# A fixed order of instructions for the first eleven head pairs of a fused attention, gate and mixer kernel

## The chip, the cores and the metric

One core of one Trainium2 chip runs the whole program. The metric is the device time of one execution in microseconds (us): the median of 3 executions of the kernel before is 831.82 us (831.67 to 832.71).

## What is computed

Three blocks follow each other, all in float32 (weights arrive as float64 words). B = 4, 12 heads, S = 448, head size 64, model width 768.

```python
scores = scale * np.matmul(q, k.transpose(0, 1, 3, 2)) - np.log(S)
attn = 1.0 / (1.0 + np.exp(-scores))              # a sigmoid, no row sums
x = np.matmul(attn, v)                            # heads side by side: (B, S, 768)
gate_pre += conv_w[k][None, None, :] * xp[:, k:k + S, :]     # 5 causal taps
x = (1.0 / (1.0 + np.exp(-gate_pre))) * (x @ w_val) @ w_out
h = np.maximum(x.transpose(0, 2, 1) @ w_tok1, 0.0) @ w_tok2
u = x + h.transpose(0, 2, 1)
out = u + np.maximum(u @ w_ch1, 0.0) @ w_ch2
```

## The kernel before

The heads are worked on in pairs: 24 pairs, six to a batch. For pair i, `scores` (L201) multiplies k by q in four chunks (8 matmuls in the program; the trace counts each as two) into a PSUM tile `pss` of which there are two, and ScalarE turns each chunk into a sigmoid tile `a` (L209, 128x896, four buffers). `av` (L212) multiplies v by the four chunks into `psy`, ScalarE copies the result to `x` (L221), and a DMA stores it to a scratch in device memory (L222). `x_back` (L224) loads it again as `xb`, with four columns of padding in front, two buffers. `post_pair` (L230) then makes of `xb` two things: its two halves in the reduced float32 format that the dense matmuls read (`split`, L88: high part on ScalarE L89, low part on VectorE L95), and the gate before its sigmoid: one tap on ScalarE (L237), four on VectorE (L239), the sigmoid at L243.

The weights are decoded on the chip. `fetch` loads 768 KB of float64 words as `raw` (three buffers), and `decode` (L104) makes a high and a low part of them in eight steps: two masks and a sum on VectorE (L110, L112, L113), a rebase of the exponent on ScalarE (L111), a merge on VectorE (L116), the high part on ScalarE (L119), an exponent mask and the low part on VectorE (L120, L121). Eighteen tiles are decoded in this phase: six of w_val, six of w_out (128x768), four of w_tok1 (128x256) and two of w_tok2 (128x448). The convolution's 30 columns `cw` are decoded as well. The tiles `dec_a` have two buffers, `dec_c` has one.

The order on each engine comes from a scheduler: it takes the instructions in the order in which they are written as priorities, models their times, and fills an engine's gaps with whatever is ready in its model. On the chip each engine then runs its list strictly in order. `PLAN` (L24) says what is written beside which pairs: pairs 0 to 10 stand alone (the lead), then the projections of batch 0 (`dense_steps`) are woven between the pairs from 11 on. `DEC_AT` (L33) says how many tiles are decoded at each pair:

```python
DEC_AT = (1, 1, 1, 1, 1, 1, 0, 0, 0, 0, 1, 2, 2, 2, 3, 2)
POST_FROM = 5
```

Behind the pairs come the channel mixer's matmuls (`ch1`, L479, and `ch2`, L491), the largest part of the program.

Of the kernel before, what the change touches and what calls it, by code (L numbers as in the profile page):

```python
# [31 lines left out]

DEC_AT = (1, 1, 1, 1, 1, 1, 0, 0, 0, 0, 1, 2, 2, 2, 3, 2)  # L33

# [4 lines left out]
def tile_kernel(ctx, tc, qT, kT, v, w_val, conv_w, w_out, w_tok1, w_tok2, w_ch1, w_ch2, out):  # L39
# [36 lines left out]
    def f(ap):  # L76
        return ap.bitcast(F32)
# [25 lines left out]

    def decode(pool, n, raw, h_out, l_out):  # L104
# [3 lines left out]
        a = pool.tile([P, DC], I32, tag="dec_a", bufs=2, name="dec_a")[:, :n]  # L108
        c = pool.tile([P, DC], I32, tag="dec_c", bufs=1, name="dec_c")[:, :n]
        nc.vector.tensor_scalar(out=a, in0=hi, scalar1=0x7FFFFE00, scalar2=None, op0=ALU.bitwise_and)  # L110
        nc.scalar.activation(out=a, in_=a, func=AF.Relu, scale=8.0, bias=exp_b)  # L111
        nc.vector.tensor_scalar(out=c, in0=hi, scalar1=0x1FF, scalar2=None, op0=ALU.bitwise_and)  # L112
        nc.vector.scalar_tensor_tensor(  # L113
            out=c.bitcast(F32), in0=lo.bitcast(U32), scalar=2.0**-32, in1=c, op0=ALU.mult, op1=ALU.add
        )
        nc.vector.scalar_tensor_tensor(  # L116
            out=a, in0=hi, scalar=-0x80000000, in1=a, op0=ALU.bitwise_and, op1=ALU.bitwise_or
        )
        nc.scalar.activation(out=h_out, in_=a.bitcast(F32), func=AF.Copy)  # L119
        nc.vector.tensor_scalar(out=e, in0=a, scalar1=-0x800000, scalar2=None, op0=ALU.bitwise_and)  # L120
        nc.vector.scalar_tensor_tensor(  # L121
            out=l_out, in0=c.bitcast(F32), scalar=2.0**-20, in1=e.bitcast(F32), op0=ALU.mult, op1=ALU.mult
        )

# [20 lines left out]
    def dec_conv(pool):  # L145
        n = KD * KW

        def go(raw):
            h = attn.tile([P, n], F32R, tag="cwHL", bufs=1, name="cwH")
            lo = attn.tile([P, n], F32R, tag="cwL", bufs=1, name="cwL")  # L150
            decode(pool, n, raw, h, lo)
            nc.vector.tensor_tensor(out=cw, in0=f(h), in1=f(lo), op=ALU.add)

        return (lambda raw: nc.gpsimd.dma_start(raw, conv_w.bitcast(I32))), go

    def dec_tok1(pool, c):
# [7 lines left out]

        return ld, lambda raw: decode(pool, NTOK, raw, wt1H[:, c], wt1L[:, c])

    def dec_tok2(pool, c):
        def ld(raw):
            nc.gpsimd.dma_start(raw[:, : 2 * S], w_tok2[c * P : (c + 1) * P].bitcast(I32))

        return ld, lambda raw: decode(pool, S, raw, wt2H[:, c], wt2L[:, c])

    def dec_w(pool, sel, kk):
# [11 lines left out]

    def load_pair(i):
        b, p = divmod(i, NP)
# [11 lines left out]
        raw_t[i] = (q, k, t)  # L199

# [28 lines left out]

    def post_pair(i):  # L230
        p = i % NP
        x = x_t.pop(i)
        xs = both.tile([P, 2, S], F32R, tag="xs", bufs=7, name="xs")
        split(xs[:, 0], xs[:, 1], x[:, PAD:])
        xs_t[i] = xs
        acc = both.tile([P, S], F32, tag="gate", bufs=6, name="gate")
        nc.scalar.activation(out=acc, in_=x[:, :S], func=AF.Copy, scale=cw[:, p * KW : p * KW + 1])  # L237
        for t in range(1, KW):
            nc.vector.scalar_tensor_tensor(  # L239
                out=acc, in0=x[:, t : t + S], scalar=cw[:, p * KW + t : p * KW + t + 1], in1=acc,  # L240
                op0=ALU.mult, op1=ALU.add,
            )
        nc.scalar.activation(out=acc, in_=acc, func=AF.Sigmoid)  # L243
        gate_t[i] = acc

# [116 lines left out]
    def dec_go():  # L362
        if raws:
            raw, go = raws.pop(0)
            go(raw)
            dec_load()

    load_pair(0)
    dec_load()
    load_pair(1)  # L370
    dec_load()
    dec_load()
    craw = attn.tile([P, 2 * KD * KW], I32, tag="craw", bufs=1, name="craw")
# [35 lines left out]

    for c in range(NF + 1):  # L410
        scores(0, c)
    rest_of = {}
    pairs0 = PLAN[0][2]
    for b, parts, pairs in PLAN:
        weave(1.0)
# [12 lines left out]
        for n, i in enumerate(pairs):  # L428
# [14 lines left out]
            post(2 if i > pairs0[-1] else 1 if i >= POST_FROM else 0)  # L443
            weave((n + 1.0) / len(pairs))
# [145 lines left out]
```

## Time and profile before

| | |
|---|---|
| median of 3 executions | 831.82 us |
| the profiled execution, its own time | 832.21 us |
| its span (first to last instruction) | 830.3 us |
| TensorE (PE) matmuls busy | 792.5 us, 95% of the span |
| VectorE (DVE) busy | 373.8 us, 45% |
| ScalarE (ACT) busy | 295.2 us, 36% |
| moved by DMA | 80.49 MB, mean 97 GB/s |

The page also cuts the span into 40 slices of 20.8 us and gives the busy share of each engine in tenths. PE has 7, 7, 6, 8, 8, 9 and then nothing but 9 until the end; VectorE has 5, 9, 7, 9, 7 and then at most 6 for a long time; the granted TensorE clock is 9 in nearly all slices, 8 in the third and the fifth.

An engine's row in the timeline gives start, duration, engine, line, operation, out<-in, count, and in brackets how long the engine stood idle before it and what ended that. Rows of one engine overlap a little, since a new instruction starts while the last one drains; what an instruction costs its engine in a dense row is the distance to the next start.

### The profile page before, as it was taken

What the parts mean: (1) busy time and instruction counts of PE and PEld (TensorE: products, weight loads), DVE (VectorE), ACT (ScalarE), POOL (GpSimd) and SP (SyncE); (2) the same over time, 40 slices, a digit from 0 to 9 for tenths busy, and PEclk for the clock granted to TensorE, in tenths of its full rate; (3) what the DMA queues carried; (4) which work ended last, traced back from release to release, by engine and by line L of the source; (5) the groups of instructions that cost most, each with busy time, mean ns of one, the idle gap of its engine ahead of it and who ended that gap; (6) DMA issues with size and microseconds to landing.
All of it is one profiled execution on the core that took longest, in us unless ns stands there. A gap on an engine that the chain in (4) does not pass through costs nothing.

```text
span 830.3 us, 9671 instructions
## 1 busy us (share of the span) xinstructions
PE 792.5 (95%) x3776; PEld 614.3 (74%) x3776; DVE 373.8 (45%) x635; ACT 295.2 (36%) x440; POOL 34.2 (4%) x97
## 2 busy tenths in 40 slices
PE   7768899999999999999989999999999999999998
PEld 2222236567677767777978899889999999999997
DVE  5979705431265323634479589994001200030002
ACT  6768755543435433433144244451002000020000
POOL 1111100000000000000000100000000000000000
PEclk9989899999999999999999999999999999999999
DMA  8756642221213121103254244535000500041001
GB/s 277 250 187 213 180 133 78 83 69 42 96 57 100 56 67 51 46 16 120 75 191 133 77 161 156 174 131 196 1 1 14 187 0 1 1 155 35 0 1 67
DMA packets 50686, 80.49 MB, mean 97 GB/s; under 512 B 4544, under 2 KB 46032, under 8 KB 50640
## 3 DMA queue, kind: packets, MB, share of 16 engines
q1 hardware_dynamic: 47280, 65.29, 24.3%
q0 software_dynamic: 3360, 14.58, 5.2%
q8 instruction: 30, 0.49, 0.2%
q14 instruction: 16, 0.13, 0.1%
HBM read 63.34 MB, written 16.52 MB: 96 GB/s over the span
## 4 chain that ended last, share of the span: by engine, by line
PE 75%; DVE 13%; DMA 6%; issue 3%; ACT 2%; SPq 1%; POOL 0%; DVEq 0%; POOLq 0%; ACTq 0%
PE psd L264 20%; PE psh L484 18%; PE pso L498 16%; PE pss L207 7%; PE psy L219 7%; PE pst L303 3%; PE pst L316 3%; DMA raw<-w_ch 3%; DVE dec_a L116 2%; DVE dec_c L113 2%; DVE wch L121 1%; DMA raw<-w_val 1%; DVE dec_a L110 1%; DVE raw L120 1%; DVE dec_c L112 1%
## 5 line engine op out<-in xcount | busy, mean ns | idle before, releaser
L484 PE MATMUL psh<-us,wch 128*128 128x448 f32 x864 | 184.6, 366 | 0.9 <-DVE wch L121 0.5
L498 PE MATMUL pso<-r,wch 128*128 128x448 f32 x864 | 184.2, 366 | 0.6 <-ACT r L89 0.6
L484 PEld LDWEIGHTS psh<-us,wch 128*128 128x128 f32 x864 | 161.9, 188 | 16.1 <-DVE wch L121 1.3
L498 PEld LDWEIGHTS pso<-r,wch 128*128 128x128 f32 x864 | 162.1, 188 | 14.9 <-ACT r L89 1.0
L91 DVE SCALAR_TENSOR_TENSOR r<-psh,r 128x448 fp32r<-128x448 f32 x48 | 29.9, 624 | 212.9 <-ACT r L89 212.8
L207 PE MATMUL pss<-q,k 64*128 64x448 f32 x384 | 97.4, 605 | 19.7 <-ACT a L209 15.6
L89 ACT ACTIVATE r<-psh 128x448 fp32r<-128x448 f32 x48 | 26.1, 544 | 230.4 <-PE psh L484 229.9
L264 PE MATMUL psd<-gv,w 128*128 128x448 f32 x432 | 95.3, 375 | 3.2 <-ACT x2T L277 3.2
L209 ACT ACTIVATE a<-pss,bias_s 128x896 f32<-128x896 f32 x96 | 92.9, 1001 | 14.5 <-PE pss L207 14.4
L264 PEld LDWEIGHTS psd<-gv,w 128*128 128x128 f32 x432 | 80.8, 191 | 19.7 <-ACT x2T L277 4.1
L219 PE MATMUL psy<-a,v 128*64 128x448 f32 x384 | 86.8, 570 | 7.3 <-issue 6.4
L264 PE MATMUL psd<-xs,w 128*128 128x448 f32 x432 | 92.8, 370 | 0.5 <-ACT xs L89 0.5
L264 PEld LDWEIGHTS psd<-xs,w 128*128 128x128 f32 x432 | 80.2, 188 | 15.5 <-issue 6.5
L207 PEld LDWEIGHTS pss<-q,k 64*128 64x128 f32 x384 | 35.0, 196 | 71.5 <-issue 34.3
L219 PEld LDWEIGHTS psy<-a,v 128*64 128x64 f32 x384 | 26.6, 142 | 58.3 <-issue 52.9
L239 DVE SCALAR_TENSOR_TENSOR gate<-xb,cw,gate 128x448 f32<-128x448 f32 x96 | 64.6, 681 | 8.9 <-ACT gate L237 7.7
L111 ACT ACTIVATE dec_a<-dec_a,exp_b 128x768 int32<-128x768 int32 (+3 forms) x43 | 37.2, 869 | 37.6 <-DVE dec_a L110 35.0
L272 DVE TENSOR_TENSOR gate<-psd,gate 128x448 f32<-128x448 f32 x24 | 15.0, 624 | 69.7 <-PE psd L264 69.4
L116 DVE SCALAR_TENSOR_TENSOR dec_a<-raw,dec_a 128x768 int32<-128x768 int32 (+2 forms) x42 | 37.2, 886 | 1.6 <-ACT dec_a L111 1.6
L113 DVE SCALAR_TENSOR_TENSOR dec_c<-raw,dec_c 128x768 f32<-128x768 uint32 (+2 forms) x42 | 37.3, 889 | 0.9
L278 DVE COPY x2T<-x2T 128x64 f32<-128x64 f32 x24 | 4.6, 193 | 62.1 <-ACT x2T L277 62.1
L303 PE MATMUL pst<-x,wt1H 128*128 128x384 f32 x112 | 30.2, 338 | 0.6 <-DVE x L290 0.6
(64 smaller groups left out, 546.9 us busy)
## 6 DMA issues: line engine op xcount, KB each, us to landing
raw<-w_ch SPq DMA_DIRECT2D x24, 768.0 KB, 4.4
q<-qT SPq DMA_DIRECT2D x24, 224.0 KB, 2.7
k<-kT SPq DMA_DIRECT2D x24, 224.0 KB, 3.4
xscr<-x SPq DMA_DIRECT2D x24, 224.0 KB, 2.6
xb<-xscr SPq DMA_DIRECT2D x24, 224.0 KB, 2.5
uscr<-x2T POOLq DMA_DIRECT2D x24, 224.0 KB, 2.2
u<-uscr SPq DMA_DIRECT2D x24, 224.0 KB, 4.1
ur<-uscr SPq DMA_DIRECT2D x24, 224.0 KB, 3.5
```

The costliest lines, as they stand in the source:

```text
L91: nc.vector.scalar_tensor_tensor(out=l_out, in0=src, scalar=0.0, in1=f(h_out), op0=ALU.max, op1=ALU.subtract)
L111: nc.scalar.activation(out=a, in_=a, func=AF.Relu, scale=8.0, bias=exp_b)
L113: nc.vector.scalar_tensor_tensor(out=c.bitcast(F32), in0=lo.bitcast(U32), scalar=2.0**-32, in1=c, op0=ALU.mult, op1=ALU.add)
L116: nc.vector.scalar_tensor_tensor(out=a, in0=hi, scalar=-0x80000000, in1=a, op0=ALU.bitwise_and, op1=ALU.bitwise_or)
L207: nc.tensor.matmul(ps[:, j, :S], k[rows, at : at + P], q[rows], start=True, stop=True)
L209: nc.scalar.activation(out=a, in_=ps[:, :, :S], func=AF.Sigmoid, bias=bias_s, scale=QK_SCALE)
L219: nc.tensor.matmul(y[cols, :S], vn[:, c, cols], a[:, j], start=c == 0, stop=c == NF)
L239: nc.vector.scalar_tensor_tensor(out=acc, in0=x[:, t : t + S], scalar=cw[:, p * KW + t : p * KW + t + 1], in1=acc, op0=ALU.mult, op1=ALU.add,)
L264: nc.tensor.matmul(ps[:, :S], w(a, kk), s[:, c, :], start=kk == 0 and n == 0, stop=kk == KD - 1 and n == 2,)
L303: nc.tensor.matmul(ps[:, :HALF], a, x[:, m], start=n == 0, stop=n == len(mm) - 1)
L484: nc.tensor.matmul(ps[:, :S], wch[fc][:, 0, a, kk * P : (kk + 1) * P], us_t[b, kk][:, c, :], start=kk == 0 and n == 0, stop=kk == KD - 1 a ...
L498: nc.tensor.matmul(acc[j][:, :S], wch[fc][:, 1, a, j * P : (j + 1) * P], r[:, c, :], start=fc == 0 and n == 0, stop=fc == KF - 1 and n == 2,)
```

## The change

The body of the loop over pairs 0 to 10 is written out in a function `lead` under a manual schedule: its instructions keep the order in which they are written on every engine. `decode` and `post_pair` are split into parts so that a part can be written later than the part it depends on: the high part of a decode and the sigmoid of a gate are put into a list `after` and issued in the next pair. `DEC_AT` gives no tile to pairs 0 to 10 any more (the first six, of w_val, are in `lead`), and the other twelve to pairs 11 to 15. `load_pair` is split in two around `av`. The decode of the convolution's columns moves from ahead of the first pair to pair 3, `x_back` of pair 0 to pair 4, and `post` of pair 0 to pair 5. Everything behind pair 10 keeps its code and the scheduler.

```diff
-DEC_AT = (1, 1, 1, 1, 1, 1, 0, 0, 0, 0, 1, 2, 2, 2, 3, 2)
+DEC_AT = (0,) * 11 + (2, 2, 2, 3, 3)
+DEC_FIRST = 6
+CONV_AT = 3
...
+    def lead():
+        nonlocal back
+        after = []
+        dec_load()
+        for c in range(NF + 1):
+            scores(0, c)
+        dec_load()
+        for i in pairs0:
+            load_qk(i + 2)
+            av(i)
+            load_v(i + 2)
+            for c in range(NF + 1):
+                scores(i + 1, c)
+            behind, after = after, []
+            if i < DEC_FIRST:
+                raw, go = raws.pop(0)
+                masks, rebase, low, high = go(raw)
+                masks()
+                rebase()
+                for fn in behind:
+                    fn()
+                low()
+                after.append(high)
+                dec_load()
+            else:
+                for fn in behind:
+                    fn()
+            if i == CONV_AT - 1:
+                cld(craw)
+            if i == CONV_AT:
+                for part in cgo(craw):
+                    part()
+            posts.append(i)
+            if i >= POST_FROM and posts[0] < NP:
+                first, last = post_parts(posts.pop(0))
+                first()
+                after.append(last)
+            if i + 1 >= POST_FROM and back < NP:
+                x_back(back)
+                back += 1
+        for fn in after:
+            fn()
+
+    with tc.manual_schedule():
+        lead()
+    for b, parts, pairs in PLAN[1:]:
```

In `masks` stand L110, L112 and L113 of before, in `rebase` L111, in `low` L116, L120 and L121, in `high` L119; in `first` the split and the five taps of a post, in `last` its sigmoid.

What this does to the lists. On SP, the queue that issues most DMAs, before, from the third pair's loads on (`xscr<-x` stores a pair's result, `xb<-xscr` loads one back):

```order
L192 DMA q<-qT 128x448
L193 DMA k<-kT 128x448
L222 DMA xscr<-x 128x448
L195 DMA v<-v 128x3x128
L198 DMA v<-v 64x128
L227 DMA xb<-xscr 128x448
L192 DMA q<-qT 128x448
```

and after, around the first load back of an `xb`:

```order
L255 DMA xscr<-x 128x448
L225 DMA v<-v 128x3x128
L228 DMA v<-v 64x128
L260 DMA xb<-xscr 128x448
L216 DMA q<-qT 128x448
L217 DMA k<-kT 128x448
```

Before, the load back stood right behind the store of the same pair, ahead of the next pair's q; now the first one stands behind the store of pair 4 and fetches pair 0.

On ACT before, in the third and fourth pair (`a<-pss` are the sigmoids of scores, `dec_a<-dec_a` the rebase, `w_n_0<-dec_a` the high part of tile n of w_val, `x<-psy` the copy of a pair's result):

```order
L119 ACTIVATE w_2_0_99<-dec_a 128x768
L119 ACTIVATE w_3_0_101<-dec_a 128x768
L89 ACTIVATE xs<-xb 128x448
L221 ACTIVATE x<-psy 128x448
L111 ACTIVATE dec_a<-dec_a,exp_b 128x768
L237 ACTIVATE gate<-xb,cw 128x448
L209 ACTIVATE a<-pss,bias_s 128x896
L119 ACTIVATE w_4_0_103<-dec_a 128x768
L209 ACTIVATE a<-pss,bias_s 128x896 x2
```

and after, from the sigmoids of pair 6 to the first ones of pair 8 (`w_n_0` with the numbers 107 and up are of w_out):

```order
L242 ACTIVATE a<-pss,bias_s 128x896 x4
L123 ACTIVATE dec_a<-dec_a,exp_b 128x768
L136 ACTIVATE w_4_0_103<-dec_a 128x768
L91 ACTIVATE xs<-xb 128x448
L272 ACTIVATE gate<-xb,cw 128x448
L254 ACTIVATE x<-psy 128x448
L123 ACTIVATE dec_a<-dec_a,exp_b 128x768
L242 ACTIVATE a<-pss,bias_s 128x896 x3
L136 ACTIVATE w_0_0_107<-dec_a 128x768
L242 ACTIVATE a<-pss,bias_s 128x896
L136 ACTIVATE w_5_0_105<-dec_a 128x768
L280 ACTIVATE gate<-gate 128x448
```

Before, the split of pair 0 (`xs<-xb`) stood ahead of the copy of pair 1; now it stands behind the sigmoids of pair 6. The first rows are the fixed order; the rebase and the high part of `w_0_0_107` are written behind the lead, and the scheduler has put them into gaps of it, the latter between two sigmoids of pair 7.

On DVE after, from the last tile of w_val to the first of w_out (before, the same kinds of rows alternate from the third tile on):

```order
L127 SCALAR_TENSOR_TENSOR dec_a<-raw,dec_a 128x768
L116 TENSOR_SCALAR dec_a<-raw 128x768
L130 TENSOR_SCALAR raw<-dec_a 128x768
L131 SCALAR_TENSOR_TENSOR w_5_1_106<-dec_c,raw 128x768
L97 TENSOR_TENSOR xs<-xb,xs 128x448
L274 SCALAR_TENSOR_TENSOR gate<-xb,cw,gate 128x448
L117 TENSOR_SCALAR dec_c<-raw 128x768
L274 SCALAR_TENSOR_TENSOR gate<-xb,cw,gate 128x448
L118 SCALAR_TENSOR_TENSOR dec_c<-raw,dec_c 128x768
L274 SCALAR_TENSOR_TENSOR gate<-xb,cw,gate 128x448
L127 SCALAR_TENSOR_TENSOR dec_a<-raw,dec_a 128x768
```

The first `xs<-xb` on DVE stood behind three tiles of w_val before; now all six tiles of w_val precede it, and the six of w_out come among the posts of pairs 0 to 4.

## Rows read from the trace of the kernel before

**Rows 1.** Windows: us, then busy us of each engine, granted clock, DMA share, GB/s.

```profile
40.00:60.00 20.00, 13.68 (x56) 4.64 (x56) 13.91 (x23) 12.31 (x18) 3.03 (x6) 0.83 0.53 181
60.00:80.00 20.00, 15.70 (x68) 4.92 (x64) 19.90 (x32) 17.13 (x25) 3.82 (x8) 0.91 0.69 218
100.00:120.00 20.00, 18.58 (x90) 6.37 (x88) 1.02 (x3) 12.93 (x16) 0.40 (x2) 1.00 0.42 132
```

**Rows 2.** Timeline of PE: where av of pair 0 ends, and where that of pair 4 does.

```profile
12.94 1.77 PE L207 MATMUL pss<-q,k 64*128 64x448 f32 x8
...
58.77 1.77 PE L207 MATMUL pss<-q,k 64*128 64x448 f32 x8
```

**Rows 3.** Waits up to 121 us: who waited for whom, us in total, times, longest.

```profile
ACT xs L89 <- DMA xb<-xscr: 7.9, 2, 5.8
...
DVE dec_a L110 <- DMA raw<-w_tok: 2.6, 3, 1.5
```

**Rows 4.** Timeline of PE: pair 11, its scores and av, and the first projection.

```profile
113.67 1.77 PE L207 MATMUL pss<-q,k 64*128 64x448 f32 x8
...
117.71 3.23 PE L219 MATMUL psy<-a,v 128*64 128x448 f32 x16
120.87 1.77 PE L207 MATMUL pss<-q,k 64*128 64x448 f32 x8
122.58 3.77 PE L264 MATMUL psd<-xs,w 128*128 128x448 f32 x17
```

**Rows 5.** Timeline of ACT in pair 11: its four sigmoids.

```profile
114.80 1.91 ACT L209 ACTIVATE a<-pss,bias_s 128x896 f32<-128x896 f32 x2 [0.47 <-PE pss L207]
116.99 1.91 ACT L209 ACTIVATE a<-pss,bias_s 128x896 f32<-128x896 f32 x2 [0.28 <-PE pss L207]
```

**Rows 6.** Timeline of ACT in a dense stretch.

```profile
58.05 0.67 ACT L237 ACTIVATE gate<-xb,cw 128x448 f32<-128x448 f32 x1
58.60 0.84 ACT L119 ACTIVATE w<-dec_a 128x768 fp32r<-128x768 f32 x1
59.34 0.93 ACT L111 ACTIVATE dec_a<-dec_a,exp_b 128x768 int32<-128x768 int32 x1
60.16 0.54 ACT L221 ACTIVATE x<-psy 128x448 f32<-128x448 f32 x1
```

**Rows 7.** Timeline of DVE in a dense stretch.

```profile
62.80 0.67 DVE L239 SCALAR_TENSOR_TENSOR gate<-xb,cw,gate 128x448 f32<-128x448 f32 x1
63.40 0.95 DVE L116 SCALAR_TENSOR_TENSOR dec_a<-raw,dec_a 128x768 int32<-128x768 int32 x1
64.27 0.55 DVE L110 TENSOR_SCALAR dec_a<-raw 128x768 int32<-128x768 int32 x1
64.74 0.55 DVE L120 TENSOR_SCALAR raw<-dec_a 128x768 int32<-128x768 int32 x1
65.32 0.96 DVE L121 SCALAR_TENSOR_TENSOR w<-dec_c,raw 128x768 fp32r<-128x768 f32 x1
```

**Rows 8.** Timeline of all engines: decoding the convolution's columns, from the first mask to the high part.

```profile
4.39 0.18 DVE L110 TENSOR_SCALAR dec_a<-craw 128x30 int32<-128x30 int32 x1 [4.39 <-DMA craw<-conv_w]
...
5.25 0.23 ACT L119 ACTIVATE cwH<-dec_a 128x30 fp32r<-128x30 f32 x1 [0.26 <-DVE dec_a L116]
```

**Rows 9.** Groups of DVE by form up to 101 us: busy us, mean ns of one.

```profile
L113 DVE SCALAR_TENSOR_TENSOR dec_c<-raw,dec_c 128x256 f32<-128x256 uint32 x4 | 1.7, 426 | 0.1
```

**Rows 10.** DMA issues: queue, operation, count, KB each, median us from issue to landing.

```profile
raw<-w_ch SPq DMA_DIRECT2D x24, 768.0 KB, 4.4
...
raw<-w_out POOLq DMA_DIRECT2D x6, 768.0 KB, 5.1
```

**Rows 11.** The tile `raw` up to 105 us: its loads' landings.

```profile
DMA to landing us min/median/max: 3.1/5.0/7.6
```

**Rows 12.** Timeline of PE: one av in the decoding stretch.

```profile
74.33 4.44 PE L219 MATMUL psy<-a,v 128*64 128x448 f32 x16
```

**Rows 13.** Windows, columns as in Rows 1: the projections of batch 0 by w_val.

```profile
120.87:163.60 42.73, 42.73 (x205) 26.93 (x203) 17.98 (x29) 22.47 (x33) 0.92 (x6) 1.00 0.26 82
```

More of the change, by code (lines that the diff above doesn't have):

```diff
@@ L102, in fetch, with decode_parts @@
         return raw
-    def decode(pool, n, raw, h_out, l_out):
+    def decode_parts(pool, n, raw, h_out, l_out):
         w = raw[:, : 2 * n].rearrange("p (n t) -> p n t", t=2)
@@ L107, in decode @@
         e = raw[:, :n]
[L108 to L115, printed above, removed]
@@ L126, in tile_kernel, with high, decode @@
+        def high():
+            nc.scalar.activation(out=h_out, in_=t["a"].bitcast(F32), func=AF.Copy)
+        return masks, rebase, low, high
+    def decode(*args):
+        for part in decode_parts(*args):
+            part()
     wts = tc.alloc_tile_pool(name="wts", bufs=1, side="right")
@@ L150, in go, with total @@
             lo = attn.tile([P, n], F32R, tag="cwL", bufs=1, name="cwL")
-            decode(pool, n, raw, h, lo)
-            nc.vector.tensor_tensor(out=cw, in0=f(h), in1=f(lo), op=ALU.add)
+            masks, rebase, low, high = decode_parts(pool, n, raw, h, lo)
+            def total():
+                high()
+                nc.vector.tensor_tensor(out=cw, in0=f(h), in1=f(lo), op=ALU.add)
+            return masks, rebase, low, total
         return (lambda raw: nc.gpsimd.dma_start(raw, conv_w.bitcast(I32))), go
@@ L169, in ld @@
             nc.gpsimd.dma_start(raw[:, : 2 * S], w_tok2[c * P : (c + 1) * P].bitcast(I32))
-        return ld, lambda raw: decode(pool, S, raw, wt2H[:, c], wt2L[:, c])
+        return ld, lambda raw: decode_parts(pool, S, raw, wt2H[:, c], wt2L[:, c])
     def dec_w(pool, sel, kk):
@@ L233, in post_pair, with first, last @@
         xs = both.tile([P, 2, S], F32R, tag="xs", bufs=7, name="xs")
-        split(xs[:, 0], xs[:, 1], x[:, PAD:])
-        xs_t[i] = xs
         acc = both.tile([P, S], F32, tag="gate", bufs=6, name="gate")
[L237 to L244, printed above, removed]
+        xs_t[i], gate_t[i] = xs, acc
+        def first():
+            split(xs[:, 0], xs[:, 1], x[:, PAD:])
+            nc.scalar.activation(out=acc, in_=x[:, :S], func=AF.Copy, scale=cw[:, p * KW : p * KW + 1])
+            for t in range(1, KW):
+                nc.vector.scalar_tensor_tensor(
+                    out=acc, in0=x[:, t : t + S], scalar=cw[:, p * KW + t : p * KW + t + 1], in1=acc,
+                    op0=ALU.mult, op1=ALU.add,
+                )
+        def last():
+            nc.scalar.activation(out=acc, in_=acc, func=AF.Sigmoid)
+        return first, last
+    def post_pair(i):
+        for part in post_parts(i):
+            part()
     carry = []
@@ L408, in mark @@
         val_done = b
-    for c in range(NF + 1):
-        scores(0, c)
     rest_of = {}
     pairs0 = PLAN[0][2]
-    for b, parts, pairs in PLAN:
+    def lead():
[29 more added lines that the diff above has]
+                for part in cgo(craw):
+                    part()
+            posts.append(i)
[11 more added lines that the diff above has]
+    for b, parts, pairs in PLAN[1:]:
         weave(1.0)
```

62 lines of the change are left out of this document (39 added, 23 removed).

## The prediction

> **What bounds the kernel now.** Start with the busy shares over time, in the table of the page: PE is busy nine tenths or more in every slice behind the sixth, and six to nine tenths before. So the time that can be won lies in the first 120 us, and what is won there moves everything behind it forward. The windows say why [rows 1]: from 60 to 80 us VectorE is busy 19.90 of 20 us and PE 15.70, while from 100 to 120 us, with the decoding done, VectorE does almost nothing and PE is busy 18.58. The timeline then gives the pace. Call A-n the moment at which the av of pair n ends and the scores of the next pair begin. A-0 is at 12.94 and A-4 at 58.77, so four pairs took 45.8 us, 11.5 us each [rows 2]. Free of other work a pair takes 120.87 - 113.67 = 7.2 us [rows 4]: A-10 is at 113.67, A-11 at 120.87. Part of the early excess is no work at all: in the list of waits ScalarE stands 7.9 us, once 5.8 us, at the split of an `xb` that is still being loaded [rows 3], with the sigmoids that PE needs queued behind it. It stands there because the load back follows the store of the same pair at once, as the list of SP shows. Every projection needs A-11 behind it, in both kernels: their PE lists agree from there on but for stray first matmuls. So I compute A-11 after the change.
>
> **Pairs 0 to 4: PE sets the pace.** The reach-back to `xb` moves: pair 0 is split behind the sigmoids of pair 6, over a pair after its load was issued, so this wait goes. Start with A-0 at 12.94 as before; the loads ahead of it only lose a w_val tile that stood between them. In a free pair the four sigmoids end at 116.99 + 1.91 - 113.67 = 5.2 us after A [rows 4, 5]. Behind them the new list has a rebase, 60.16 - 59.34 = 0.82 us, and the high part of the tile before, 59.34 - 58.60 = 0.74 us [rows 6], which end at 6.8, ahead of A at 7.2. The masks that the rebase waits for are done by then: their load was issued a pair or more ahead, and VectorE has only one decode to do in such a pair. So these pairs cost 7.2 us each; the ends I keep are 7.2 and the 11.5 of before, and I take the lower since nothing in the list waits for a fresh transfer. **The convolution's columns** are decoded at pair 3, where before they were done during the first loads. There ScalarE must wait for VectorE in order: rebase of tile 3 until 6.05 after A-3, then on VectorE merge 0.87, mask 0.58 and low part 0.87 [rows 7] until 8.4, then the short chain from the first mask to the high part, 5.25 + 0.23 - 4.39 = 1.1 us [rows 8], to 9.5. The copy of x takes 0.5 more [rows 6], so the first sigmoid of pair 5 starts at 10.0 in place of 7.2 + 1.1 = 8.3 [rows 5]: I charge 1.7 us. A-5 = 12.94 + 5 x 7.2 + 1.7 = 50.6.
>
> **Pairs 6 to 11: VectorE sets the pace.** The scheduler fills the six w_out tiles and the first w_tok1 tiles into these pairs, beside the posts of pairs 0 to 4. Counted in the new VectorE list, the first split is reached when tile 5 of w_val is through: sigmoids 5.2, rebase 0.82, merge 0.87, a mask 0.47, two steps 0.58 and 0.87, which is 8.8 us behind A-5, at 59.4. From there to the merge of the second w_tok1 tile, on which a sigmoid of pair 11 waits on ScalarE, stand:
> - 5 posts of 5 instructions, 0.60 each by the distance of a gate step to the next start [rows 7]; the split is of that size: 15.0 us.
> - 6 tiles of w_out, each with two masks of 0.47, one step of 0.58 and three of 0.87 [rows 7]: 4.13 us; the first lacks one mask, already counted: 24.3 us.
> - A w_tok1 tile: its long step takes 426 ns [rows 9] where a w_out tile's takes 950, so 0.45 x 4.13 = 1.9 us, and 1.4 us of the next one: 3.3 us.
>
> That is 42.6 us, to 102.0. Behind it ScalarE still has a small high part (0.3) and a sigmoid (1.0), and PE the last quarter of an av, 3.23 / 4 = 0.8 [rows 4]: 104.1. The lists cross between ScalarE and VectorE twice a tile with little to spare; nothing in the old trace shows this pattern, so the hand-offs lie between 0 and 5 us (three late landings of 1.5 us, the longest wait on a w_tok load [rows 3]); I take 0.8, nearer to zero, since from 60 to 80 us the same kinds of rows kept VectorE busy 99% [rows 1]. **A-11 is then 104.9, 16.0 us earlier.**
>
> **What is pushed behind A-11.** Some 9 us of VectorE work that was done by 101 us now lies behind A-11: a w_tok1 tile, two w_tok2 tiles (448/768 of 4.13 each), the four gate steps of pair 5. It shares the next 42.7 us with the projections, in which VectorE was busy 18.0 us [rows 13], so there is room for it; the two ends are 0 and 9 us, and I take 0.4 for sigmoids of pair 12 that stand behind the w_tok2 tiles on ScalarE. If that cover were gone, the third projection would wait for the first one's PSUM tile. Later pairs and the channel matmuls keep their lists.
>
> **The sum.** 16.0 - 0.4 = 15.6 us off. The profiled execution took 832.21 us with a span of 830.3; it becomes 816.6. The median of the runs is 0.4 lower, so I forecast **816.2 us**.
>
> **Two rules of the Trainium skill.** The w_out loads are issued on POOL while VectorE works. In the trace such a load of 768 KB lands after 5.1 us, against 4.4 us for those of the same size from SP [rows 10]: the price is 0.7 us, and the list has 1 us or more to spare in most places. The Trainium skill, SBUF — State Buffer, section "A bandwidth-pool intuition that's wrong (but worth ruling out)", says that a transfer issued from that engine can wait for its descriptors until VectorE releases a shared port: 620 ns alone, about 3100 ns beside a copy. By that page each load would land an estimated 2.5 us later, and the sum would be about 820 us in place of 816; that is the rival of late loads below, and the 0.7 us of the trace speaks against it.
>
> **Rivals.**
> - *Late loads.* There are three `raw` buffers, so a tile's load is issued when the tile three before it is decoded. The third w_out tile has 7.6 us of VectorE work between, the sixth 6.4, the third w_tok1 tile 5.1; at the median landing of 5.1 all are in time, at the longest of 7.6 [rows 11] they are 0, 1.2 and 2.5 us late. Price 3.7 us: 819.9. For it: VectorE waited for such loads three times before [rows 3]. Chance 0.13.
> - *A slow TensorE clock.* If VectorE sets the pace, PE has gaps in pairs 6 to 11. From 40 to 60 us, with PE busy 13.7 of 20 us, the mean granted clock was 0.83, a mix of the levels 1.2 and 2.4 GHz, and an av of that stretch took 4.44 us in place of 3.23 [rows 1, 4, 12]. If none of this is hidden behind VectorE, five pairs lose 1.2 us each: 822.2. Against it: ScalarE is 1.5 us late at the start of these pairs anyway. The Trainium skill, TensorE: Matmul & The Clock Gate, section "HAM oscillation", says that a matmul engine left waiting for data falls to the lower rate each time anew, which would put the time at this rival; the 0.83 of the old trace agrees that it happens in this stretch. Chance 0.09.
> - *The backlog is not hidden.* 9 us of VectorE work less the 1.77 + 3.77 us [rows 4] after which the first projection's result is there to be multiplied, 3.5 us: 819.7. Chance 0.06.
> - *PE all the way.* If VectorE can run ahead, all eleven pairs take 7.2 us: A-11 at 12.94 + 79.2 + 1.7 = 93.8, 27.0 us off, 804.8. Against it stand 42.6 us of VectorE work in five pairs of 36 us, in a fixed order. Chance 0.06.
> - *Slower: one load at a time.* If the loads of w_out don't overlap (each issue stands on POOL behind paddings of `xb` and `v` that wait for VectorE or PE), a tile costs its landing and its decoding, 5.1 + 4.13 = 9.2 us; six of them from 59.4 on (55.2), plus 3.3 and 2.1, and a landing of 7.6 for half of them, 7.5 more: A-11 at 127.5, 6.6 us later than before, and with the 0.4 behind it 839 us. It decides from 2.7 us of waiting per tile on, 16.0 / 6. Against it: the three buffers, and a VectorE without gaps from 60 to 80 us in the old trace [rows 1] with the same loads. Chance 0.03.
> - *The fixed order is not there:* the lists show that it is, except for the w_out tiles in its gaps, which I have counted. No chance of its own.
>
> **How the numbers follow.** The forecast has 0.63; late loads 0.13, clock 0.09, backlog 0.06, PE all the way 0.06, one load at a time 0.03. The range 811 to 823 holds the forecast with its bounds (hand-offs of 0 to 5 us: 815.4 to 820.4; early pairs a little better or worse than 7.2) and the three rivals between 819 and 823; it leaves out 0.09. A measurement of this kernel tells 0.2%, 1.7 us, from no change. Slower by more than that has the 0.03 of the slower rival, within it 0.02 from mixtures of it with others, faster 0.95.
>
> **What would show it.** Right: A-1 to A-4 7.2 us apart in the timeline of PE; no wait of ScalarE for `xb`; VectorE busy 95% or more from about 59 to 102 us, and pairs 6 to 11 at 9 us; the first projection (17 or so matmuls of `psd`) at 106 to 108 us in place of 122.6; the stretch from there to the end as long as before within 1 us. Wrong: early pairs at 9 us or more, with ScalarE waiting for a mask or PE for q or v; VectorE waiting for `raw` more than 5 us in all; PE waiting in the 40 us behind the first projection.

## The result: 818.5 us, 1.6% less

The median of 4 executions of the changed kernel is 818.48 us (815.96 to 820.14), that of the kernel before in the same comparison 831.75 us (829.27 to 832.71): a ratio of 0.984, 95% interval 0.981 to 0.988. Forecast were 816.2 us, with a range of 811 to 823. The profiled execution took 819.66 us with a span of 817.9; the forecast on that footing was 816.6. One execution of a kernel below (the posts earlier) took 1547 us and is left out of its times and its ratio.

The windows that answer to [rows 1], of the changed kernel (us, then busy us of PE, PEld, DVE, ACT, POOL, granted clock, DMA share, GB/s):

```profile
40.00:60.00 20.00, 17.61 (x78) 5.90 (x76) 11.82 (x22) 14.67 (x21) 2.29 (x7) 0.91 0.70 226
60.00:80.00 20.00, 15.87 (x67) 5.09 (x65) 19.93 (x32) 17.12 (x24) 3.59 (x7) 0.91 0.73 228
100.00:120.00 20.00, 19.26 (x92) 10.52 (x92) 18.57 (x47) 16.92 (x28) 3.43 (x8) 1.00 0.64 187
```

From 40 to 60 us PE does 17.6 us of work where it did 13.7; from 60 to 80 us VectorE is as full as it was; from 100 to 120 us VectorE, once idle, is full too, with the work that now lies behind A-11.

The timeline of PE of the changed kernel, answering to [rows 2, 4]: the starts of the scores behind A-0, A-4, A-5, A-11, the middle of pair 5, the end of pair 11 and the first projection:

```profile
12.81 1.77 PE L240 MATMUL pss<-q,k 64*128 64x448 f32 x8
...
41.61 1.77 PE L240 MATMUL pss<-q,k 64*128 64x448 f32 x8
45.35 2.56 PE L240 MATMUL pss<-q,k 64*128 64x448 f32 x8 [1.97 <-ACT a L242]
47.84 4.23 PE L252 MATMUL psy<-a,v 128*64 128x448 f32 x16
52.01 1.77 PE L240 MATMUL pss<-q,k 64*128 64x448 f32 x8
...
103.31 1.02 PE L240 MATMUL pss<-q,k 64*128 64x448 f32 x4 [0.39 <-ACT a L242]
104.26 3.23 PE L252 MATMUL psy<-a,v 128*64 128x448 f32 x16
107.42 1.77 PE L240 MATMUL pss<-q,k 64*128 64x448 f32 x8
109.12 3.51 PE L306 MATMUL psd<-xs,w 128*128 128x448 f32 x16
```

Pairs 1 to 4 take (41.61 - 12.81) / 4 = 7.2 us each, where they took 11.5. Pair 5 takes 10.4. A-11 is at 107.42 in place of 120.87, 13.45 us earlier; forecast was 104.9. From A-11 to the end of the span are 710.5 us in place of 709.4. So the whole gain lies ahead of A-11, as the prediction had it.

The windows of the changed kernel pair by pair, from A-n to A-n+1, first pairs 1 to 5 together, then 6 to 11 (columns as above):

```profile
12.81:52.01 39.20, 35.56 (x163) 12.02 (x161) 21.33 (x35) 29.28 (x36) 5.16 (x11) 0.96 0.72 230
52.01:59.21 7.20, 6.78 (x35) 2.35 (x33) 3.38 (x6) 6.33 (x9) 1.00 (x3) 1.00 0.72 246
59.21:68.38 9.17, 7.00 (x34) 2.28 (x33) 9.10 (x15) 7.41 (x11) 1.61 (x4) 1.00 0.62 188
68.38:79.29 10.91, 8.95 (x35) 2.80 (x33) 10.91 (x18) 9.96 (x15) 2.05 (x4) 0.84 0.79 249
79.29:87.31 8.02, 6.90 (x34) 2.36 (x32) 6.84 (x11) 7.22 (x10) 1.74 (x4) 1.00 0.86 289
87.31:99.77 12.46, 8.96 (x35) 2.81 (x33) 12.05 (x20) 9.43 (x14) 1.39 (x4) 0.86 0.47 139
99.77:107.42 7.65, 6.91 (x34) 2.38 (x33) 7.45 (x24) 7.03 (x12) 2.26 (x6) 1.00 0.81 223
```

Until A-6 VectorE is half idle and PE nearly full. In pairs 7 to 11 it is VectorE that is full, but for one gap, which the timeline of DVE shows (the first split of a post, the first mask behind the gap, the merge of the first w_tok1 tile, and the two merges of the second and third, of which the prediction counted to the second's):

```profile
60.99 0.62 DVE L97 TENSOR_TENSOR xs<-xb,xs 128x448 fp32r<-128x448 f32 x1
...
87.65 0.60 DVE L116 TENSOR_SCALAR dec_a<-raw 128x768 int32<-128x768 int32 x1 [1.49 <-DMA raw<-w_out]
...
101.49 0.42 DVE L127 SCALAR_TENSOR_TENSOR dec_a<-raw,dec_a 128x256 int32<-128x256 int32 x1
...
104.03 0.75 DVE L127 SCALAR_TENSOR_TENSOR dec_a<-raw,dec_a 128x256 int32<-128x256 int32 x2
```

From 60.99 to the end of the second tile's merge, at about 104.4, are 43.4 us. Forecast were 42.6 of work and 0.8 of hand-offs: 43.4. ScalarE no longer waits for `xb` in this stretch (7.9 us before, [rows 3]).

### The profile page after: what moved, and what is told of

It is laid out like the page before. It is cut to its first block, busy times and chain, and to the rows that moved or that the text cites. A ratio compares the mean times of both kernels' runs of the same rounds, so it can differ in the third digit from the quotient of the medians.

```text
span 817.9 us, 9669 instructions
## 1 busy us (share of the span) xinstructions
PE 789.1 (96%) x3776; PEld 613.5 (75%) x3776; DVE 373.0 (46%) x635; ACT 294.7 (36%) x440; POOL 34.3 (4%) x97
## 4 chain that ended last, share of the span: by engine, by line
PE 71%; DVE 17%; DMA 6%; ACT 3%; issue 2%; POOL 0%; SPq 0%; ACTq 0%; DVEq 0%; POOLq 0%
PE psd L306 17%; PE psh L568 17%; PE pso L582 16%; PE pss L240 7%; PE psy L252 6%; PE pst L345 3%; PE pst L358 3%; DMA raw<-w_ch 3%; DVE dec_a L127 2%; DVE gate L274 2%; DVE dec_c L118 2%; DVE wch L131 2%; DVE raw L130 2%; DVE dec_a L116 1%; ACT a L242 1%
## 5 line engine op out<-in xcount | busy, mean ns | idle before, releaser
L252 PE MATMUL psy<-a,v 128*64 128x448 f32 x384 | 84.8, 564 | 1.1 <-POOL xb L259 1.1
L118 DVE SCALAR_TENSOR_TENSOR dec_c<-raw,dec_c 128x768 f32<-128x768 uint32 (+2 forms) x42 | 37.5, 893 | 0.9
```

The costliest lines, as they stand in the source:

```text
L118: nc.vector.scalar_tensor_tensor(out=c.bitcast(F32), in0=lo.bitcast(U32), scalar=2.0**-32, in1=c, op0=ALU.mult, op1=ALU.add)
L252: nc.tensor.matmul(y[cols, :S], vn[:, c, cols], a[:, j], start=c == 0, stop=c == NF)
```

## The experiments

Each kernel is the changed one with the edit shown; "ahead of A-11" means ahead of the sigmoids of pair 11 in ScalarE's list. The ratio in each is to the kernel before, run on the same chip. The texts of expectations call a kernel by the label that stands in brackets behind its heading. From "All eleven pairs in fixed order" on, all kernels also decode the columns first.

**The columns decoded first (e1).**

```diff
     cld, cgo = dec_conv(dec)
+    cld(craw)
+    for part in cgo(craw):
+        part()
...
-            if i == CONV_AT - 1:
-                cld(craw)
-            if i == CONV_AT:
-                for part in cgo(craw):
-                    part()
```

> The changed kernel with one part undone: the convolution's columns are decoded ahead of the first pair, as in the kernel before. Theory (the stall at pair 3 holds ScalarE for 1.6 us, PE then falls to a lower granted clock, and both come on top of a chain that VectorE sets from there on): pair 5 takes 7.2 us in place of 10.4, A-5 comes at 48.8 in place of 52.0, A-11 at about 104.2 in place of 107.4, the time is 815 to 816 us. Rival (VectorE's total work up to A-11 sets the end, so that an early stall is absorbed): A-5 moves, A-11 stays at 107, the time stays at 818.

Measured: 814.90 us (814.32 to 815.83), ratio 0.980 [0.978, 0.982]. A-0 comes at 13.32, 0.5 later; then all of pairs 1 to 6 take 7.2 us, A-5 is at 49.32 in place of 52.01, and A-11 at 104.33 in place of 107.42. The columns at pair 3 cost some 3 us, not 1.7.

**What the stand of PE costs beyond itself (e7).** A stand of PE is a wait in which it has nothing to do. The timeline of ACT of the changed kernel shows where the one of pair 5 comes from: the short chain waits 1.97 us for VectorE, and the first sigmoid of pair 5 starts at 44.30, 2.69 us behind A-4, where a free pair has it 1.1 behind [rows 4, 5].

```profile
43.16 0.32 ACT L123 ACTIVATE dec_a<-dec_a,exp_b 128x30 int32<-128x30 int32 x1 [1.97 <-DVE dec_a L116]
...
43.88 0.53 ACT L254 ACTIVATE x<-psy 128x448 f32<-128x448 f32 x1
44.30 1.90 ACT L242 ACTIVATE a<-pss,bias_s 128x896 f32<-128x896 f32 x2
```

That is 1.6 late, what the prediction charged. But PE stood from 43.4 to 45.35, and behind that its granted clock was a mix of the two levels of 1.2 and 2.4 GHz for almost 5 us (windows of the changed kernel):

```profile
45.30:47.90 2.60, 2.54 (x10) 0.67 (x10) 1.04 (x2) 1.91 (x3) 0.00 (x0) 0.73 0.90 323
47.90:50.00 2.10, 2.10 (x8) 0.71 (x8) 0.18 (x1) 2.04 (x3) 0.00 (x0) 0.52 1.14 296
```

To tell the clock from the stand, PE got work in it:

```diff
                 scores(i + 1, c)
+                if i == CONV_AT + 1 and c == 1:
+                    fill(4)
```

> The changed kernel with eight more matmul instructions at most (four in the program) whose product nobody reads, on PE between the second and third quarter of the scores of pair 5, where PE stands for 1.7 us for the sigmoid behind the convolution's columns. If the lower granted clock behind that stand is what made pair 5 10.4 us long instead of 8.8: granted clock 1.0 from 45 to 50 us, the pss of pair 5 at 1.92 us and the av at 3.23, pair 5 at 8.8 to 9.0 us, A-5 at 50.4 to 50.7; and the first split on VectorE comes earlier by the same 1.5 us. Rival (ScalarE is late for longer than I read, the clock is only a sign of it): pair 5 stays at 10.2 to 10.6 us. The whole: 817 us if the 1.5 us is kept, 818.5 if VectorE and ScalarE lose it again in pairs 6 to 11.

The same windows with the filler:

```profile
45.30:47.90 2.60, 2.60 (x12) 1.21 (x13) 0.73 (x1) 1.60 (x3) 0.00 (x0) 1.00 0.87 316
47.90:50.00 2.10, 2.10 (x14) 0.86 (x12) 0.40 (x1) 2.10 (x3) 0.00 (x0) 1.00 1.06 307
```

The clock is 1.00, the av takes 3.23 us in place of 4.23, and pair 5 takes 9.36 us (41.27 to 50.63) in place of 10.40. I had expected 8.8 to 9.0: the filler runs past the stand, so 1.0 us is what it gained and less than what the clock cost. The cost itself can be read from the kernel whose steps stand at once (e4, below), which has the columns at the same place and a stand of the same length, behind which the granted clock stayed at 1.00 in its profile (timeline of PE, from the middle of its pair 5 to A-5; its A-4 is at 41.31):

```profile
45.11 1.92 PE L240 MATMUL pss<-q,k 64*128 64x448 f32 x8 [2.03 <-ACT a L242]
46.96 3.23 PE L252 MATMUL psy<-a,v 128*64 128x448 f32 x16
50.12 1.77 PE L240 MATMUL pss<-q,k 64*128 64x448 f32 x8
```

There pair 5 takes 8.81 us (41.31 to 50.12): 7.2 and the 1.6 of ScalarE. So the clock cost the changed kernel 1.6 us in this pair of its profiled execution, and a stand of 2 us does not bring it down each time; what decides it stays open. The time with the filler is 817.23 us (815.78 to 818.38), ratio 0.982 [0.980, 0.984], too near to 818.48 to say that the whole kept it, though A-11 in its profile is at 104.64.

**The order left to the scheduler (e2).** `lead` without the manual schedule, all other edits kept:

```diff
-    with tc.manual_schedule():
-        lead()
+    lead()
```

> The changed kernel's text without the manual schedule around the lead, so that the scheduler orders it. Theory (the gain of the early pairs is the xb wait, and the scheduler put the split of pair 0 ahead of a copy of x because its model thought xb was there): the split is hoisted to the third pair again, ScalarE waits for xb 5 us or more in all, A-4 comes at 50 us or later in place of 41.6, and the time is 826 to 834 us. Rival (it is the later decoding, or the parts written a pair behind, not the fixed order): A-4 at about 42, 817 to 820 us.

Measured: 832.57 us (829.21 to 836.62), ratio 1.001 [0.999, 1.003]. A-4 is at 52.50. The parts, the moved columns and the moved loads are together worth nothing without the fixed order. (The next run shows that the fixed order is worth little without the steps written a pair behind.) The list of waits of this kernel up to 123 us has the old row again, since its scheduler takes the first split of a post back to 22.8 us:

```profile
PE pss L240 <- ACT a L242: 24.4, 17, 5.9
...
ACT xs L91 <- DMA xb<-xscr: 8.0, 4, 4.7
```

**The steps at once, not a pair behind (e4).** The fixed order stays, but the high part stands right behind the low part and the gate's sigmoid right behind its steps:

```diff
-                after.append(high)
+                high()
...
-                after.append(last)
+                last()
```

> The changed kernel with its lag undone: the high part of a tile right behind its low part, the sigmoid of a gate right behind its taps, in the same pair and the same fixed order. Theory: in pairs 1 to 5 nothing is lost, since ScalarE has 1.4 us free between its rebase and the next copy of x and the merge ends in that time (7.2 us a pair); in pairs 6 to 11 ScalarE waits about 3 us a pair for the four taps ahead of the copy of x, of which the pace of VectorE hides a part: A-11 at 110 to 118, 821 to 829 us. Rival (the lag does nothing where VectorE sets the pace): A-11 at 107, 817 to 819 us.

Measured: 829.39 us (827.62 to 832.47), ratio 0.997 [0.996, 0.999]. Pairs 1 to 4 still take 7.2 us, so the early pairs owe nothing to the lag. Pairs 6 to 11 take 12.2 on the mean (A-5 at 50.12, A-11 at 123.06), with ScalarE waiting for VectorE in order (waits up to 124 us):

```profile
PE pss L240 <- ACT a L242: 22.0, 13, 4.2
...
ACT gate L280 <- DVE gate L274: 10.9, 3, 4.6
ACT w L136 <- DVE dec_a L127: 9.2, 8, 2.9
```

So the lag is worth 11 us, and all of it where a pair has posts. Both figures lie beyond what I expected (A-11 at 110 to 118, 821 to 829 us): the waits for VectorE were under-sized. Without the lag the fixed order alone takes 2.6 us off the 831.97 of the kernel before; fixed order and lag together take 13.3.

**Less work on VectorE, first try (e3).** For the w_out tiles the sum (L118) is left out:

```diff
-            nc.vector.scalar_tensor_tensor(
-                out=c.bitcast(F32), in0=lo.bitcast(U32), scalar=2.0**-32, in1=c, op0=ALU.mult, op1=ALU.add
-            )
+            if add:
+                nc.vector.scalar_tensor_tensor(
+                    out=c.bitcast(F32), in0=lo.bitcast(U32), scalar=2.0**-32, in1=c, op0=ALU.mult, op1=ALU.add
+                )
```

> Leaves out one VectorE step, the sum of the low bits, of each of the six w_out tiles: 6 x 0.87 = 5.2 us of VectorE work in pairs 6 to 11, and nothing on another engine. Theory (VectorE sets the pace there): A-11 comes 4 to 5.5 us earlier, 102 to 103.5, the time is 813 to 814.5. Rival (the transfers of raw, or ScalarE and PE with its lower clock, set the pace): A-11 within 1.5 us of 107.4, 817 to 819 us.

Measured: 818.29 us (815.61 to 820.95), ratio 0.984 [0.981, 0.987]: a miss. A-11 was at 107.32, as before the edit. The scheduler had filled the room: the third and fourth tiles of w_tok1 and the first steps of w_tok2 now stood ahead of A-11, and VectorE waited 2.52 us once for a w_out load, with PE's clock down behind it (4.63 us of standing, then chunks of scores at half their pace). I took from it that the filling of gaps costs the late pairs and not VectorE's amount of work. The list had changed with the amount, so this run alone could not tell; the next three do.

**All eleven pairs in fixed order (e5).** Columns first, and a tile decoded in each pair, so that w_out tiles are no longer left to the gaps; four of them then stand ahead of A-11, not six and the first of w_tok1:

```diff
-DEC_FIRST = 6
+DEC_FIRST = 11
```

> The convolution's columns are decoded ahead of pair 0 (as in e1) and the fixed order decodes a tile in each of the eleven pairs (tiles 6 to 10 are w_out), so no w_out tile is left to the gaps. Theory (the decodes that the scheduler fills between the sigmoids cost the late pairs, and not VectorE's amount of work): pairs 1 to 5 at 7.2 us, then six pairs with a tile and a post each, in which ScalarE has 5.2 + 0.82 + 0.74 + about 1.5 us of a post = 8.3 us; A-11 at 13.3 + 5 x 7.2 + 6 x 8.3 = 99, against 104.3 in e1; about 809.5 us. Rival (VectorE's amount sets the pace, as the prediction had it: 25 us of w_out tiles and 15 us of posts from A-5 on): A-11 stays at 103 to 105, about 814 to 815 us. Rival (the turn-around of the three raw buffers): VectorE waits for raw more than 4 us in all and A-11 is at 102 or later.

Measured: **803.82 us** (803.59 to 804.16), ratio 0.966 [0.964, 0.968]. A-5 is at 48.61, A-11 at 93.78, earlier than I expected of any theory. Its windows in pairs 9 and 10:

```profile
70.64:78.33 7.69, 6.78 (x34) 2.35 (x33) 7.48 (x12) 7.25 (x11) 1.63 (x3) 1.00 0.77 248
78.33:86.05 7.72, 6.78 (x34) 2.35 (x32) 7.51 (x12) 7.28 (x11) 1.64 (x3) 1.00 0.79 265
```

ScalarE's 8.3 us a pair were mis-sized (7.3). And the full engine is VectorE: a tile and a post occupy it for the 7.72 us of the pair, as its timeline shows (first mask of a tile, the split, the first mask of the next):

```profile
75.83 0.58 DVE L116 TENSOR_SCALAR dec_a<-raw 128x768 int32<-128x768 int32 x1
...
80.25 0.62 DVE L97 TENSOR_TENSOR xs<-xb,xs 128x448 fp32r<-128x448 f32 x1
80.79 2.84 DVE L274 SCALAR_TENSOR_TENSOR gate<-xb,cw,gate 128x448 f32<-128x448 f32 x4
83.55 0.60 DVE L116 TENSOR_SCALAR dec_a<-raw 128x768 int32<-128x768 int32 x1
```

VectorE waits for no `raw` from A-5 on, so the rival of the three buffers did not come either. The theory of the gaps gave the right direction for a reason that this does not show: there were fewer tiles ahead of A-11 too. So, with the same fixed order, only the number of tiles was changed, in both directions.

**More tiles ahead of A-11 (e9).** Here `TILES` replaces `DEC_FIRST`, and the tiles of a pair follow each other, each high part one tile behind:

```diff
-DEC_FIRST = 6
+TILES = (1,) * 6 + (2, 1, 2, 1, 0)
...
-            if i < DEC_FIRST:
+            for _ in range(TILES[i]):
```

> As e5 (columns first, decodes in the fixed order, posts from pair 5 on), but all six w_out tiles stand ahead of the sigmoids of pair 11, two of them in one pair twice, as many as the scheduler puts there in the changed kernel; in e5 only four do. So the order is fixed, nothing fills gaps, and only the amount of VectorE's work ahead of A-11 differs from e5. If VectorE's amount sets the end of these pairs (the prediction's step): two tiles more at 4.42 us each as e5 shows them (75.83 to 80.25 us), so A-11 at 93.8 + 8.8 = 102.6, between 101 and 105, about 812 us or, with less left behind A-11, 810. If it is the filling of gaps that costs (my reading after e3), and not the amount: A-11 at 96 to 98, pairs 7 to 11 at 8 us or less on the mean.

Measured: 811.62 us (811.48 to 812.50), ratio 0.975 [0.971, 0.978]. A-5 is at 49.44 and A-11 at 104.96: 55.5 us for six pairs, against 45.2 in the kernel with four tiles. Two tiles more are 8.8 us of VectorE; the scheduler put two w_tok1 tiles beside them as well (I had written that nothing would fill gaps), so 9 to 13 us of VectorE's work cost 10.3. And the kernel with the columns first, with the same work in the gaps, took 55.0 us from A-5 to A-11. In this pair of kernels filling gaps costs nothing that can be seen; the amount does, as the first theory had it.

**No w_out tile ahead of A-11 (e8).** The six follow in fixed order behind the last pair of `lead`:

```diff
+        for _ in range(6):
+            raw, go = raws.pop(0)
+            masks, rebase, low, high = go(raw)
...
```

> As e1, with the six tiles of w_out in the fixed order behind the last pair of it, so none is decoded before A-11 begins. Theory (gap-filled decodes cost the late pairs): pairs 6 to 11 have four sigmoids and a post, 6.7 us on ScalarE, so PE sets the pace: 7.2 us each, A-11 at 13.3 + 11 x 7.2 = 92.5. Behind it VectorE has 25 us of w_out and 9 us of backlog beside the 18 us it had from 121 to 164 us: 52 us in a stretch of 42.7, so about 10 us come back later; about 811 to 815 us in all. Rival (nothing but PE and posts sets the late pairs in e1, the decodes are harmless): A-11 at 103 or later.

Measured: 814.93 us (811.72 to 815.23), ratio 0.978 [0.976, 0.981]. All pairs take 7.2 us and A-11 is at 91.78, but the 42.7 us behind it have become VectorE's (windows of this kernel):

```profile
48.59:91.78 43.19, 40.69 (x194) 14.11 (x192) 23.49 (x36) 36.63 (x50) 3.30 (x14) 1.00 0.63 196
91.78:134.50 42.72, 40.07 (x188) 25.51 (x187) 41.28 (x74) 29.39 (x44) 7.20 (x14) 1.00 0.52 162
```

From A-11 to the end of the span are 718.1 us, 10.0 more than with four tiles ahead; and the profiled execution, of 811.72 us, is the fastest of the four by 3 us. Together (the middle columns are of the profiled executions, of 819.66, 815.83, 811.48, 803.72 and 811.72 us):

| w_out tiles ahead of A-11 | A-5 | A-11 | A-5 to A-11 | A-11 to the end | median |
|---|---|---|---|---|---|
| 6 and w_tok1, the changed kernel | 52.01 | 107.42 | 55.4 | 710.5 | 818.48 |
| the same, columns first | 49.32 | 104.33 | 55.0 | 709.8 | 814.90 |
| 6 and w_tok1, fixed order | 49.44 | 104.96 | 55.5 | 704.7 | 811.62 |
| 4, fixed order | 48.61 | 93.78 | 45.2 | 708.1 | 803.82 |
| 0, fixed order | 48.59 | 91.78 | 43.2 | 718.1 | 814.93 |

The fixed order with six tiles gains 5 us behind A-11 over the row above it because PE already did four short pieces of the projections while it waited (1.29, 1.28, 1.28 and 1.71 us of `psd` between 65 and 91 us).

**The posts earlier (e6, e6b).** As with all in fixed order, but with the first post at pair 2:

```diff
-POST_FROM = 5
+POST_FROM = 2
```

> As e5, with the posts three pairs earlier (the first one at pair 2 in place of pair 5, each xb still loaded a pair ahead of its split). Theory: ScalarE's list sets the pace of a pair that has a tile and a post (8.3 us) and PE that of the others (7.2), so it does not matter which six pairs have both: A-11 at 98 to 100, as in e5, 809 to 810 us; pairs 3 to 8 are the long ones. Rival (early pairs have no room, since the load of xb collides with q, k, v): pairs 3 to 8 at 9 us or more and ScalarE waits for xb, A-11 at 103 or later. If VectorE's amount set the pace, spreading it over ten pairs in place of six would be what helps, and e6 would be 4 us or more faster than e5.

> The kernel of e6 again, for its profile (that of e6 was of an execution in which all of PE ran at half its rate, 1545 us, and tells nothing). Its times were 2.4 us above those of e5. Theory: pairs 3 to 8 at 7.7 us, as pairs 7 to 11 of e5, the others at 7.2, so A-11 at 93 to 95 as in e5 and the 2.4 us lie behind A-11. Rival (early pairs have less room, loads of xb beside q, k, v and w_val): one or more of pairs 3 to 8 at 8.5 us or more, A-11 at 96.

Measured: 806.1 us (805.39 to 806.50; ratio 0.968 [0.967, 0.970]), and 805.96 again (two executions, 805.20 and 806.73; 0.967 [0.963, 0.972]). In the profile of the second, five pairs, 5 to 9, take 7.66, 7.73, 7.68, 7.72 and 8.15 us, the others 7.2, and A-11 is at 94.68. That is the size I expected, a pair or two later than I wrote: a post beside a tile costs its half microsecond in whichever pair it stands, and starting earlier gains nothing. It loses, rather: against the posts from pair 5 on, the profiles (806.73 and 803.72 us) show 0.9 us more ahead of A-11 and 2.1 more behind it. Why behind it, stays open.

**The same work, other order (e10).** All in fixed order, with a post's four gate steps between the decoding steps of the next tile:

```diff
-                masks()
+            masks(taps[:3])
...
-                low()
+                low(rest[:2])
```

> As e5, with the same instructions in another fixed order: the four gate steps of a post stand between the decoding steps of the next tile on VectorE, and its split between the last two; on ScalarE the two copies of the post stand ahead of the high part. In e5 a gate step that follows another on the same tile starts 0.69 us after it, in the changed kernel 0.60 with another instruction between. If VectorE's list sets the pace of e5's pairs 7 to 11 (7.72 us each, VectorE busy 7.51): some 0.4 us less a pair, 7.3 us, where ScalarE's 7.3 us of busy time comes in; A-11 at 92.0 to 92.6, 802 to 802.6 us. Rival (ScalarE's list or the hand-offs set the pace): pairs stay at 7.7 or get longer since the merge stands behind more steps, 803.8 us or more. Rival (nothing of it shows behind A-11, because the work pushed there sets the pace): A-11 at 92.3 and still 803.8 us.

Measured: 804.37 us (803.55 to 804.96), ratio 0.966 [0.962, 0.969]. The pairs 8 to 11 take 7.46 us each, not 7.72. VectorE's list shows why, and why it is not 7.3: a gate step costs 0.60 between other steps (70.64 to 71.23), while in the kernel without the change three of a post's four steps stand behind a step on the same tile and cost 0.72 (of the 2.76 us from 80.79 to 83.55 above, the last step took 0.60). The 0.69 of my expectation is the mean of the four. And now VectorE waits for ScalarE:

```profile
70.64 0.68 DVE L302 SCALAR_TENSOR_TENSOR gate<-xb,cw,gate 128x448 f32<-128x448 f32 x1
71.23 0.56 DVE L140 TENSOR_SCALAR raw<-dec_a 128x768 int32<-128x768 int32 x1
...
77.22 0.98 DVE L135 SCALAR_TENSOR_TENSOR dec_a<-raw,dec_a 128x768 int32<-128x768 int32 x1 [0.44 <-ACT dec_a L130]
```

So VectorE's list did set the 7.72, and at 7.46 ScalarE's takes over (in its list only 0.29 us a pair are idle, for PE). A-11 is at 93.26, 0.5 earlier although the first pair ended 0.4 later; in the whole time it can't be told from the kernel without it. The fastest version is thus the one with all eleven tiles in fixed order and the columns first, 803.8 us, 14.7 less than the changed kernel.

## Why the prediction was right

**Pairs 0 to 4, 7.2 us each:** right to the hundredth, and the wait for `xb` is gone. But the gain of these pairs is kept only because of the lag in the later ones: without it A-11 was at 123.06, with the early pairs as fast.

**The columns, 1.7 us:** the stall was read rightly (1.6 us), but pair 5 is 3.2 us over 7.2: the other 1.6 are the lower clock behind PE's stand, which the term put at nothing. The kernel without the lag had the same stand, a granted clock of 1.00 and 8.81 us in place of 10.40. The prediction had a clock rival, but for pairs 6 to 11, not here (and the av of 4.44 us by which it priced that rival lies at 74.33 [rows 12], not in the stretch from 40 to 60 us that it named). The Trainium skill, TensorE: Matmul & The Clock Gate, section "HAM oscillation", describes a kernel whose matmul engine waits for data in every round and falls to the lower rate each time anew. Here it was not each time: the clock fell behind a stand of 1.97 us, did not behind one of 2.03 in the kernel without the lag, and did not behind the stands of 0.42 us in each early pair.

**VectorE sets the pace of pairs 6 to 11, 42.6 + 0.8 us:** right, to 43.4, and that the figures agree is in part luck: 1.49 us were one late load, of the sixth w_out tile (the rival of late loads had 1.2 for it; the rest of its 3.7 did not come), so the work was 41.9 and the hand-offs nothing. The experiments bear the step out: more tiles or fewer ahead of A-11 move it by about VectorE's time for them, until PE's 7.2 us is reached. My doubt after the run without the sum was wrong.

**The tail, 2.1 us:** it was 3.0, and another chain. The last sigmoid held nothing up: PE ran from 103.31 to 107.42 without a wait, the last chunk of scores and the av, and what it had waited for before was the sigmoid of the second chunk. That sigmoid stands behind the high part of the first w_tok1 tile, and so behind that tile's merge, at 101.49 (rows of ScalarE in the changed kernel):

```profile
101.94 0.42 ACT L136 ACTIVATE wt1H<-dec_a 128x256 fp32r<-128x256 f32 x1
102.27 0.99 ACT L242 ACTIVATE a<-pss,bias_s 128x896 f32<-128x896 f32 x1
```

So A-11 hung on the merge of the first w_tok1 tile, which ended at 101.9, with 5.5 us of ScalarE and PE behind it, and not on that of the second, to which the prediction counted. (Here ScalarE and PE, coming from A-10, were there within 0.2 us of it; in the kernel with the columns first ScalarE waits 1.38 us for that merge, and A-11 again comes 5.5 us behind it.) VectorE's amount was right, the place where the chain leaves VectorE was one tile too late, and the two errors of the path nearly cancel. I had ended the pair with the last quarter of an av; here the whole av and its last scores came behind ScalarE's last hold-up.

**Behind A-11, 0.4 us:** it was 1.05. The backlog rival (3.5) did not come, but its mechanism is there: at 129.33 PE waits 1.42 us for a sigmoid, since ScalarE waited for the gate steps of posts left behind. The rows of ScalarE, and the one of PE, in the changed kernel:

```profile
122.37 0.58 ACT L280 ACTIVATE gate<-gate 128x448 f32<-128x448 f32 x1 [2.51 <-DVE gate L274]
...
127.81 0.58 ACT L280 ACTIVATE gate<-gate 128x448 f32<-128x448 f32 x1 [1.58 <-DVE gate L274]
128.29 0.99 ACT L242 ACTIVATE a<-pss,bias_s 128x896 f32<-128x896 f32 x1
...
129.33 1.02 PE L240 MATMUL pss<-q,k 64*128 64x448 f32 x4 [1.42 <-ACT a L242]
```

In sum: 1.5 for the columns with the clock, 0.2 at the first split, 0.9 in the tail and 0.65 behind A-11, less 0.1 for an A-0 that came earlier, are the 3 us by which the profiled execution is over 816.6. Of the signs that the prediction named, two came out against it in a small size: the first projection is at 109.12, not at 106 to 108, and PE does wait once in the 40 us behind it. And the 1.7 us that it took a measurement to tell apart are less than the 4.2 by which the executions of the changed kernel differ.

**The slow clock in pairs 6 to 11** came (0.84 and 0.86 in pairs 8 and 10) and cost little beyond what VectorE took anyway, as the prediction argued: VectorE's list has no gap from 60.99 to 104.4 but the 1.49 us for the load. **One load at a time** did not come. Nor do the medians show the price of the port: w_out loads, issued on POOL, landed after 5.6 us, w_val loads from POOL, issued while VectorE was about half idle, after 5.5, and from SP, in the first 15 us, after 6.5 (the DMA issues of the changed kernel, KB each, median us to landing):

```profile
raw<-w_out POOLq DMA_DIRECT2D x6, 768.0 KB, 5.6
raw<-w_val SPq DMA_DIRECT2D x3, 768.0 KB, 6.5
raw<-w_val POOLq DMA_DIRECT2D x3, 768.0 KB, 5.5
```

The Trainium skill, SBUF — State Buffer, section "A bandwidth-pool intuition that's wrong (but worth ruling out)", gives about 3100 ns in place of 620 for a transfer issued on POOL beside a VectorE copy, an estimated 2.5 us more. Here the four w_out loads issued while VectorE was full (61 to 80 us) took 5.0 to 7.5 us, 6.0 in the median, 0.5 more than those of w_val from POOL. The 7.5 are the late load of the sixth tile; whether the port had a part in that was not tried.

**What the prediction did not see:** the "PE all the way" rival was put aside because of 42.6 us of VectorE work. Right for this kernel, but two tiles and the w_tok1 tiles need not have stood there; behind A-11 VectorE was idle for more than half of 42.7 us [rows 13]. That is where most of the further 14.7 us lay; the columns are the rest.

## What to carry to other kernels

When an engine sets the pace of a stretch, count not only its work but what of it must lie ahead of the event that everything waits for, and put the rest where that engine idles: with two w_out tiles and the w_tok1 tiles moved behind A-11 the kernel went to 803.8 us from 811.6 (fixed order) or 814.9 (gaps), with all six moved it went back to 814.9. Where in-order engines cross twice for one item, a fixed order pays together with steps that are written one item behind their cause: either alone left 829.4 or 832.6 us, both 818.5. And an experiment that takes work away from an engine tests nothing while a scheduler may fill the room; fix the order first.

## What the hardware showed

Behind a stand of PE of 1.97 us in an otherwise full stretch the granted clock was 0.52 to 0.73 for nearly 5 us, 1.6 us on top of the stand; behind stands of 0.42 us it stayed at 1.00. But it also stayed at 1.00 behind stands of 2.03 us (at 45.11) and 2.98 us (at 118.05) in the kernel without the lag, so the length of a stand alone does not decide. The changed kernel, with such stands, spreads by 4 us from run to run (815.96 to 820.14; mean granted clock 0.998 in the fastest and 0.992 in the two slowest), the one in fixed order without them by 0.6 us (803.59 to 804.16; clock 0.999 to 1.000); that the one causes the other was not tried. On VectorE a 128x448 gate step that needs the result of the one right ahead of it starts 0.72 us after it, and 0.60 with an independent one between.
